# Moving products apart: an attention pair in the mixing stage and the second routing of a mixture-of-experts kernel on one Trainium2 core

## The chip, the cores and the metric

The kernel runs on 1 core of one Trainium2 chip. The time is device microseconds of one execution; three executions of the kernel before gave 1412.86, 1415.44 and 1416.71 us, median 1415.44. One more execution was recorded by the profiler. PE is TensorE's matmul stream, PEld its weight loads, DVE is VectorE, ACT is ScalarE, POOL is GpSimd, SP is SyncE, which here only issues DMAs.

## The reference, cut to what matters

```python
# q,k,v: [8, 8, 576, 64]; p: [8, 8, 32, 64]
pp  = softmax(p k^T / 8) v ;  a = softmax(q pp^T / 8) pp          # x = a as [8, 576, 512]
u   = x + real(fft(fft(x, axis=1), axis=2))                       # sequence, then channels
un  = (u - mean(u)) / sqrt(var(u) + 1e-6)
x   = u + relu(un @ w_ch1) @ w_ch2                                # 512 -> 2048 -> 512, the "mixing" stage
logits = x @ w_gate ; keep = sigmoid(x @ w_local) >= 0.5          # 8 experts
e[s] = e[s-1] if keep[s] and s > 0 else argmax(logits[s])         # a scan along the sequence
out[s] = softmax(logits[s])[e[s]] * (relu(x[s] @ w1[e]) @ w2[e])  # 512 -> 1024 -> 512, expert e only
```

Float32 products are made of three float16 ones (high by high, high by low, low by high: the list `PASS`).

## The kernel before, in words

**Mixing.** The eight batch rows are mixed one after another (`full(b)`, 512 of the 576 places each), and the remaining 64 places of four rows are mixed together as `R0` and `R1` (`half`). The order is 0, 1, 2, R0, 3, 4, 5, 6, R1, 7. A mix has 16 slices f: `mm1(f)` makes twelve products of 512 columns into a bank `hp`, which ACT and DVE split into halves `ht`; `mm2(f-2)` makes twelve into the accumulators `acc`. `mm1` reads the whole transposed input `UT[b]` from its first product on.

**What runs beside it.** Python generators hand out the other work in steps, one step per `yield`. `tick` is called after every third product of a full mix (a sub-tick) and advances each generator in the list `bg` by 0.25 times its rate. While mix b runs, `attention(b+1)` is handed out at rate 2.3, `last`, which is `after_mix` of the mix before (scale, halves, transpose, logits), at rate 1.2, and `expert_weights` (casts of the expert weights) at 1.3. `attention` has some 60 steps and a mix 112 sub-ticks for it; what is left is drained before the next mix begins. The tile scheduler orders the instructions of each engine by program order as priority and by readiness in its own timing model, so an instruction can be issued ahead of its place in the program. Each engine then works its instructions in the order given.

**The pair of products in question.** In `attention`, `products(cs, hf, tiles)` makes the cosine (cs 0) or sine (cs 1) product of one group of 128 columns hf into a bank `bp`. Products(0,0,...) and products(0,1,...), six matmuls each, stand in one step. `att` banks come from the pool `psA`, which has two; the logits of `after_mix` use the same pool (`lp`, read by DVE at L1208 into `lsum`). After the products the step order is halves, `zd`, three output tiles t with products `P`, `Q`, `X`, and `norm`, whose four transposed tiles are sent by DMA into `UT` (L724). Output tile 2 fills a quarter of the shared tile; its `P` and `X` hold both `att` banks.

**Routing.** The first routing (`gr` 0) runs in mix 7 and covers half of the places. The second (`finish_routing`: `after_mix` of mix 7 by TensorE transposes, then `routing(1)` = `choose` and `place`) runs at rate 1.2 beside the first expert turns. In an expert turn `e1` (96 products of 128 columns, 8 ticks) and `e2` (24 products of 512 columns, 8 ticks) alternate over consecutive blocks. `choose` sends `ff` products (places to rows, L1286 to L1293), a scan on DVE, `ep` products (L1310, L1314); `place` sends `tt` and `rk` (L1351, L1352), some 34 small DVE operations, and then nine chunks of DVE comparisons, each followed by four `tab` products (L1465). The second routing has to be done when the seventh turn begins (`drain(r1)`).

**Buffers.** `hl` has three slots in SBUF, which the rows gathered for expert blocks (`xg`) and the halves `xh` of `after_mix` share; `U` has eight, for the mixes' outputs and the experts' results `ys`.

Of the kernel before, what the change touches and what calls it, by code (L numbers as in the profile page):

```python
# [192 lines left out]
def _build(tc, nc, ctx, A, stop):  # L193
# [152 lines left out]
    def attention(b):  # L346
# [237 lines left out]

        for hf in range(2):
            products(0, hf, (0, 1))
        yield
        for hf in range(2):
            products(0, hf, (2,))
# [608 lines left out]
    def after_mix(tiles, by_pe=False):  # L1198
        xt = None

        def logits(col):
            lp = att(f"lp{col}")
            for c in range(4):
                nc.tensor.matmul(lp[:, :18], xt[:, c], wgh[:, c].rearrange("p y e -> p (y e)"), start=c == 0, stop=False,
                                 skip_group_check=True)
                nc.tensor.matmul(lp[:, :9], xt[:, 4 + c], wgh[:, c, 0], start=False, stop=c == 3, skip_group_check=True)
            lsum = wp.tile([128, 9], F32, tag="lsum", name=f"lsum{col}", bufs=2)
            nc.vector.tensor_reduce(lsum, lp[:, :18].rearrange("p (y e) -> p e y", y=2), axis=AX.X, op=ALU.add)  # L1208
            nc.vector.tensor_scalar(LG[:, col], lsum, RSC[:, col:col + 1], 2.0 ** -20, ALU.mult, ALU.mult)

        for j, (ut, col) in enumerate(tiles):
            sc = wp.tile([128, 2], F32, tag="rsc", name=f"rsc{col}", bufs=2)
            nc.vector.tensor_reduce(sc[:, 0:1], ut, axis=AX.X, op=ALU.max, apply_absolute_value=True)
            nc.vector.tensor_scalar(RSC[:, col:col + 1], sc[:, 0:1], 1e-30, 0.25, ALU.max, ALU.mult)
            nc.vector.reciprocal(sc[:, 1:2], RSC[:, col:col + 1])
            yield
            hl = wp.tile([128, 1024], F16, tag="hl", name=f"xh{col}", bufs=3)
            nc.scalar.activation(hl[:, :512], ut, AF.Copy, scale=sc[:, 1:2])
            nc.vector.scalar_tensor_tensor(hl[:, 512:], ut, sc[:, 1:2], hl[:, :512], ALU.mult, ALU.subtract)
            yield  # L1220
            if j:
                yield
                logits(tiles[j - 1][1])
                yield
            xt = wp.tile([128, 8, 128], F16, tag="xt", name=f"xt{col}", bufs=1)
            if by_pe:
                for x in range(2):
                    turn_half(xt[:, 4 * x:4 * x + 4], hl[:, 512 * x:512 * x + 512], f"xtp{col}_{x}", x)
            else:
                nc.sync.dma_start_transpose(out=xt, in_=hl)  # L1230
            nc.sync.dma_start(XS[128 * col:128 * col + 128], hl)
            yield
        for _ in range(1 if by_pe else 4):
            yield
        logits(tiles[-1][1])
        yield


    def wait(n):
        for _ in range(n):  # L1240
            yield

    def choose(gr, rp):

# [28 lines left out]
        for k in range(2):  # L1273
            nc.vector.tensor_tensor(mr[:, k], fk[:, k, 16:18].unsqueeze(2).to_broadcast([128, 2, 4]),
                                    rmask.unsqueeze(1).to_broadcast([128, 2, 4]), op=ALU.mult)
        yield from wait(2)
        fs = rp.tile([4, 2, 576], F16, tag="fs", name=f"fs{gr}")
        for k in range(2):
            for lu in range(2):
                ps = att(f"ff{gr}_{k}_{lu}")  # L1280

                def sel(t):
                    return fk[:, k, 0:16].rearrange("p (b s) -> p s b", s=4)[:, 2 * t + lu]

                if lu == 0:
                    nc.tensor.matmul(ps[:4, 0:128], sel(0), idh, start=True, stop=True, skip_group_check=True)  # L1286
                    nc.tensor.matmul(ps[:4, 128:256], sel(1), idh, start=False, stop=True, skip_group_check=True)
                    nc.tensor.matmul(ps[:4, 256:288], mr[:, k, 0], i32r, start=False, stop=True, skip_group_check=True)
                else:
                    nc.tensor.matmul(ps[:4, 33:161], sel(1), anti, start=True, stop=True, skip_group_check=True)  # L1290
                    nc.tensor.matmul(ps[:4, 161:288], sel(0), anti[:, :127], start=False, stop=True, skip_group_check=True)
                    nc.tensor.matmul(ps[:4, 0:1], sel(0), anti[:, 127:128], start=False, stop=True, skip_group_check=True)
                    nc.tensor.matmul(ps[:4, 1:33], mr[:, k, 1], i32v, start=False, stop=True, skip_group_check=True)  # L1293
                if k:
                    nc.vector.tensor_copy(fs[:, k, 288 * lu:288 * lu + 288], ps[:4, :288])
                else:
                    nc.scalar.copy(fs[:, k, 288 * lu:288 * lu + 288], ps[:4, :288])
            yield
# [4 lines left out]
        rev = bass.AP(tensor=src.tensor, offset=src.offset + 575, ap=[src.ap[0], [-1, 287]])  # L1303
        nc.vector.tensor_copy(e16[:, 1, 1:288], rev)
        nc.vector.tensor_copy(e16[:, 1, 0:1], e16[:, 0, 288:289])
        yield from wait(2)
        ep = att(f"ep{gr}")
        for t in range(2):
            for lu in range(2):
                nc.tensor.matmul(ep[:, 4 * (2 * t + lu):4 * (2 * t + lu) + 4], e16[:, lu, 128 * t:128 * t + 128],  # L1310
                                 idh[:4, :4], start=t + lu == 0, stop=True, skip_group_check=True)
        for q in range(4):
            for lu in range(2):
                nc.tensor.matmul(ep[32 * q:32 * q + 32, 16 + lu:17 + lu], e16[:, lu, 256:288], idh[:4, q:q + 1],  # L1314
                                 start=False, stop=True, skip_group_check=True)
        nc.vector.tensor_copy(EXP[:, c0:c0 + 16].rearrange("p (b k) -> p b k", k=4),
                              ep[:, 0:16].rearrange("p (k b) -> p b k", b=4))
# [10 lines left out]
        nc.vector.tensor_scalar(sm, sm, 1e-9, None, ALU.add)  # L1328
        nc.vector.reciprocal(sm, sm)
        nc.vector.tensor_tensor(d, d, OH[:, c0:c0 + 18], op=ALU.mult)  # L1330
        pe = t18("pe")
        nc.vector.tensor_reduce(pe, d, axis=AX.X, op=ALU.add)
        nc.vector.tensor_tensor(pe, pe, sm, op=ALU.mult)
        val, pc = VAL[:, c0:c0 + 18], PIECES[:, c0:c0 + 18]
        nc.vector.scalar_tensor_tensor(val, pe, 2.0 ** -28, RSC[:, c0:c0 + 18], ALU.mult, ALU.mult)
        nc.scalar.copy(pc[:, :, 0:4], c32[:, 420:564].rearrange("p (i c) -> p c i", i=4)[:, c0:c0 + 18])
        for i in range(4, 7):
            nc.vector.tensor_copy(pc[:, :, i], val)
# [4 lines left out]
    def place(nm, ncol, b0, nb, early, rp):  # L1343
# [4 lines left out]
        rk = att(f"rk{nm}")  # L1348
        tt = att(f"tt{nm}")
        ohf = oh.rearrange("p c e -> p (c e)")  # L1350
        nc.tensor.matmul(tt[:, :n8], ones, ohf, start=True, stop=True)  # L1351
        nc.tensor.matmul(rk[:, :n8], tri, ohf, start=True, stop=True)  # L1352
        tot = rp.tile([128, 8, 36], F32, tag="tot", name=f"tot{nm}")
        inc = rp.tile([128, 8, 36], F32, tag="inc", name=f"inc{nm}")
        if ncol < 36:
# [100 lines left out]
        nc.vector.tensor_scalar(pi, pi, 7, None, ALU.arith_shift_right)  # L1456
        nc.vector.tensor_copy(blk[:, 0, :ncol], pi)
        nc.vector.scalar_tensor_tensor(blk[:, 1, :ncol], blk[:, 0, :ncol], -128.0, pos, ALU.mult, ALU.add)
        yield from wait(4)

        tab = att(f"tab{nm}")
        made = []

        def table(c, ow, bv):
            nc.tensor.matmul(tab[:, :7 * nb].rearrange("p (i n) -> p i n", i=7), ow, bv[:, :, :nb],  # L1465
                             start=c == 0, stop=c == ncol - 1)

        for c0 in range(0, ncol, CT):
            cs = slice(c0, min(c0 + CT, ncol))
# [9 lines left out]
            nc.vector.tensor_tensor(ow[:, :n], iota.unsqueeze(1).to_broadcast([128, n, 128]),  # L1479
                                    blk[:, 1, cs].unsqueeze(2).to_broadcast([128, n, 128]), op=ALU.is_equal)  # L1480
            made.append((c0, n, ow, bv))
            yield
            if c0:
                m0, mn, ow, bv = made[-2]
                for i in range(mn):
# [39 lines left out]

    w1b, w2b = [], []
    xg, xt, regs, hb = {}, {}, {}, {}
    newest = [None]

    def load_x(b):  # L1530
        mp = M["p"]
# [36 lines left out]
    def e1(b, todo=(), beside=iter(())):  # L1568
# [3 lines left out]
        for fg in range(2):  # L1572
            hp = (psM, psO)[fg].tile([128, 512], F32, tag="ho"[fg], name=f"ehp{b}_{fg}")
            for f in range(4):
                n = 0
                cols = slice(128 * f, 128 * f + 128)
                for c in range(4):
                    for (x, y) in PASS:
                        newest[0] = nc.tensor.matmul(hp[:, cols], w1b[r][:, 2 * c + fg, x, cols], xt[b][:, 4 * y + c],  # L1579
                                                     start=n == 0, stop=n == 11, skip_group_check=True).ins  # L1580
                        n += 1
                if f % 2 == 0:
                    for fn, t in todo:
                        fn(t, 2 * fg + f // 2, 2 * fg + f // 2 + 1)
                if f % 2:
                    next(beside, None)
                if f < 3:
                    tick()
            nc.scalar.activation(ht[:, fg, 0], hp, AF.Relu)  # L1589
            nc.vector.scalar_tensor_tensor(ht[:, fg, 1], hp, 0.0, ht[:, fg, 0], ALU.max, ALU.subtract)  # L1590
            tick()
# [32 lines left out]
    def e2(b, todo=()):  # L1624
# [5 lines left out]
        for f in range(8):  # L1630
            for (x, y) in PASS:
                for a in range(2 if two else 1):
                    rows = slice(64 * a, 64 * a + 64) if two else slice(0, 128)
                    c0 = 128 * (f % 4)
                    nc.tensor.matmul(op[rows], h[:, f // 4, x, c0 + rows.start:c0 + rows.stop], w2b[r + a][:, f, y],  # L1635
                                     start=n == 0, stop=n == 23, skip_group_check=True)
                n += 1
            if f % 2 == 0:
                for fn, t in todo:
# [157 lines left out]
```

## Time and profile before

| what | value |
|---|---|
| median of three executions | 1415.44 us (1412.86 to 1416.71) |
| profiled execution | 1416.94 us, its span 1414.9 us |
| PE busy | 1368.8 us, 97% of the span |
| PEld busy | 790.2 us, 56% |
| DVE, ACT, POOL busy | 702.1, 518.4, 376.0 us |
| TensorE's granted clock | 0.991 of full speed over the span |

The span is what the profile's rows cover; the profiled execution's time is 2.0 us more. A window row gives a stretch's busy times by engine, a timeline row one instruction or a run of equal ones with its start and length, and in square brackets the idle time of the engine ahead of it with what ended it. A matmul's row is longer than the distance to the next one, because matmuls are pipelined; their rate is read from the starts of consecutive rows.

### The profile page before, as it was taken

How to read it: one execution, taken by the hardware profiler on the slowest of the kernel's cores; microseconds unless marked ns; L12 is line 12 of the kernel's file. 1: busy time of each engine (PE TensorE's matmuls, PEld its weight loads, DVE VectorE, ACT ScalarE, POOL GpSimd, SP SyncE). 2: the span in 40 equal slices, each digit the busy share in tenths (PEclk: the TensorE clock that was granted, in tenths of full speed). 3: DMA queues.
4: the chain of work that ended last, by engine and by line, in shares of the span. 5: the costliest groups of instructions: out<-in, count | busy, mean ns of one | idle time of the engine just before them, and what ended most of it. 6: DMA issues, size and time to landing. Idle time of an engine off the chain costs nothing. (4 is left out here: it accounts for less than half of the span.)

```text
span 1414.9 us, 27811 instructions
## 1 busy us (share of the span) xinstructions
PE 1368.8 (97%) x10868; PEld 790.2 (56%) x10868; DVE 702.1 (50%) x1420; ACT 518.4 (37%) x953; POOL 376.0 (27%) x386
## 2 busy tenths in 40 slices
PE   7999899999999999999999999999899999999998
PEld 5653444444564544444444456445677777776565
DVE  5899957657544655655655655443751111111111
ACT  2543365455445545445445444211211111111112
POOL 1102243443422443343343342000211121122101
PEclk7999999999999999999999999999999999999999
DMA  7475384684567657557557446243949669957883
GB/s 263 141 253 168 100 238 121 169 235 122 142 175 202 164 137 212 158 140 217 151 131 217 126 134 173 67 179 113 284 126 301 192 183 252 264 142 238 236 250 140
DMA packets 219640, 256.62 MB, mean 181 GB/s; under 512 B 151663, under 2 KB 163055, under 8 KB 216816
## 3 DMA queue, kind: packets, MB, share of 16 engines
q1 hardware_dynamic: 213424, 235.39, 58.9%
q0 software_dynamic: 6080, 19.40, 4.1%
q8 instruction: 87, 1.43, 0.4%
q14 instruction: 49, 0.40, 0.1%
HBM read 267.52 MB, written 52.95 MB: 226 GB/s over the span
## 5 line engine op out<-in xcount | busy, mean ns | idle before, releaser
L1176 PE MATMUL acc<-w,ht 128*128 128x512 f16 x1728 | 411.0, 379 | 1.0 <-ACT ht L1163 0.8
L1156 PE MATMUL hp<-ut,w 128*128 128x512 f16 (+1 forms) x1536 | 366.1, 379 | 2.2 <-DMA ut<-unh 1.6
L1156 PEld LDWEIGHTS <-w 128*128 128x128 f16 x1920 | 182.6, 98 | 180.5 <-issue 10.9
L1176 PEld LDWEIGHTS <-ht 128*128 128x128 f16 x1728 | 165.4, 98 | 190.4 <-issue 8.5
L339 POOL TENSOR_TENSOR halfs<-stage,halfs 128x512 f16<-128x512 f32 x128 | 150.5, 1181 | 298.7 <-ACT halfs L338 280.1
L1635 PE MATMUL eo<-w2b,hx 128*128 128x512 f16 (+1 forms) x984 | 207.5, 379 | 0.1
L1579 PE MATMUL ehp<-xgt,w1b 128*128 128x128 f16 x3360 | 202.6, 219 | 1.1 <-PE ehp L1579 0.8
L1579 PEld LDWEIGHTS <-w1b 128*128 128x128 f16 x3360 | 192.6, 98 | 16.5 <-issue 3.8
L1590 DVE SCALAR_TENSOR_TENSOR hx<-ehp,hx 128x512 f16<-128x512 f32 x70 | 48.2, 689 | 269.4 <-ACT hx L1589 255.7
L1164 DVE SCALAR_TENSOR_TENSOR ht<-hp,ht 128x512 f16<-128x512 f32 (+1 forms) x160 | 101.1, 632 | 149.6 <-ACT ht L1163 148.6
L1163 ACT ACTIVATE ht<-hp 128x512 f16<-128x512 f32 (+1 forms) x160 | 88.0, 550 | 238.3 <-PE hp L1156 233.4
L1635 PEld LDWEIGHTS <-hx 128*128 128x128 f16 (+1 forms) x984 | 87.3, 100 | 95.3 <-issue 3.5
L1644 POOL DMA_INDIRECT out<-ys,sidx x38 | 38.2, 1006 | 290.4 <-ACT ys L1643 268.9
L1589 ACT ACTIVATE hx<-ehp 128x512 f16<-128x512 f32 x70 | 41.8, 597 | 155.5 <-PE ehp L1579 155.5
L1643 ACT ACTIVATE ys<-eo,scl 128x512 f32<-128x512 f32 x38 | 26.1, 687 | 155.5 <-PE eo L1635 155.5
L338 ACT CAST halfs<-stage 128x512 f16<-128x512 f32 x128 | 77.6, 615 | 9.2 <-DMA WS<-halfs 5.4
L337 ACT ACTIVATE stage<-stage 128x512 f32<-128x512 f32 x128 | 77.7, 623 | 0.2
L1534 POOL DMA_INDIRECT xg<-XS,gidx x38 | 39.7, 1045 | 140.9 <-DVE sidx L1500 52.1
L364 POOL TENSOR_TENSOR qh<-q,qh 128x1420 f16<-128x1420 f32 x12 | 34.6, 2883 | 51.0 <-ACT qh L363 50.9
L1156 PE MATMUL hp<-utr,w 128*128 128x256 f16 x384 | 47.1, 272 | 0.0
L541 POOL TENSOR_TENSOR eo<-ee 128x256 f32<-128x256 f32 (+1 forms) x21 | 18.6, 887 | 74.3 <-DVE ee L525 71.1
L576 PE MATMUL bp<-cst,eh 128*128 128x289 f16 (+1 forms) x168 | 25.5, 286 | 11.5 <-DVE lsum L1208 9.8
(413 smaller groups left out, 1404.0 us busy)
## 6 DMA issues: line engine op xcount, KB each, us to landing
w1b<-WS SPq DMA_DIRECT2D x156, 512.0 KB
w2b<-WS SPq DMA_DIRECT2D x156, 512.0 KB
stage<-in_w SPq DMA_DIRECT2D x64, 512.0 KB
WS<-halfs SPq DMA_DIRECT2D x128, 256.0 KB
q<-in_qd SPq DMA_DIRECT2D x16, 710.0 KB
v<-in_vd SPq DMA_DIRECT2D x16, 640.0 KB
k<-in_kd SPq DMA_DIRECT2D x16, 576.0 KB
XS<-xh SPq DMA_DIRECT2D x36, 256.0 KB
```

What stands on the lines that cost most here:

```text
L337: nc.scalar.activation(st[:, a], st[:, a], AF.Copy, scale=64.0 if k < 4 else 256.0)
L338: nc.scalar.copy(so[:, 0], st[:, a])
L339: nc.gpsimd.tensor_tensor(so[:, 1], st[:, a], so[:, 0], op=ALU.subtract)
L1156: nc.tensor.matmul(hp[:, c0:ntok], w12[:, f, 0, x, 128 * c:128 * c + 128], ut[:, 4 * y + c, c0:ntok], start=n == 0, stop=n == 11, skip_gro ...
L1163: pace[1] = nc.scalar.activation(ht[:, 0, :ntok], hp[:, :ntok], AF.Relu).ins
L1164: pace[0] = nc.vector.scalar_tensor_tensor(ht[:, 1, :ntok], hp[:, :ntok], 0.0, ht[:, 0, :ntok], ALU.max, ALU.subtract).ins
L1176: nc.tensor.matmul(self.acc[j], ht[:, x, 128 * j:128 * j + 128], w12[:, f, 1, y], start=f == 0 and n == 0, stop=f == 15 and n == 2)
L1534: nc.gpsimd.indirect_dma_start(out=g_, out_offset=None, in_=XS[0:rows], in_offset=bass.IndirectOffsetOnAxis(ap=gidx[:, b:b + 1], axis=0), ...
L1579: newest[0] = nc.tensor.matmul(hp[:, cols], w1b[r][:, 2 * c + fg, x, cols], xt[b][:, 4 * y + c], start=n == 0, stop=n == 11, skip_group_ch ...
L1589: nc.scalar.activation(ht[:, fg, 0], hp, AF.Relu)
L1590: nc.vector.scalar_tensor_tensor(ht[:, fg, 1], hp, 0.0, ht[:, fg, 0], ALU.max, ALU.subtract)
L1635: nc.tensor.matmul(op[rows], h[:, f // 4, x, c0 + rows.start:c0 + rows.stop], w2b[r + a][:, f, y], start=n == 0, stop=n == 23, skip_group_ ...
```

## The change

In `attention`, from batch row 2 on, two empty steps stand between the first pair of products. In `after_mix` of the last mix, the halves take slots of the pool `U` in place of `hl`. In the second routing, more empty steps stand ahead of `ff`, `ep` and the tables, two in place of one after each chunk, and each of its products (`ff`, `ep`, `tt`, `rk`, `tab`) gets an ordering edge, without a semaphore, behind the expert product that was written last at that point of the program (`latest`). The first routing keeps its steps. In the diff below, the first two `wait` lines stand ahead of `ff` and of `ep`, the third ahead of the tables, and the last one after each chunk; `pe` then stands in place of `nc.tensor` in those products.

```diff
         for hf in range(2):
             products(0, hf, (0, 1))
+            if hf == 0 and b >= 2:
+                yield from wait(2)
...
-            hl = wp.tile([128, 1024], F16, tag="hl", name=f"xh{col}", bufs=3)
+            if by_pe:
+                hl = wp.tile([128, 512], F32, tag="U", name=f"xh{col}", bufs=8).bitcast(F16)
+            else:
+                hl = wp.tile([128, 1024], F16, tag="hl", name=f"xh{col}", bufs=3)
...
+    class in_line:
+        def __init__(self, late):
+            self.late = late
+        def matmul(self, *a, **k):
+            with tc.issue_after(latest[0]) if self.late and latest[0] is not None else nullcontext():
+                nc.tensor.matmul(*a, **k)
...
-        yield from wait(2)
+        yield from wait(6 if gr else 2)
...
+                pe = in_line(gr)
...
-        yield from wait(2)
+        yield from wait(5 if gr else 2)
         ep = att(f"ep{gr}")
+        pe = in_line(gr)
...
+        pe = in_line(not early)
...
-        yield from wait(4)
+        yield from wait(4 if early else 16)
...
-            yield
+            yield from wait(1 if early else 2)
...
-                        newest[0] = nc.tensor.matmul(hp[:, cols], w1b[r][:, 2 * c + fg, x, cols], xt[b][:, 4 * y + c],
+                        newest[0] = latest[0] = nc.tensor.matmul(hp[:, cols], w1b[r][:, 2 * c + fg, x, cols], xt[b][:, 4 * y + c],
...
-                    nc.tensor.matmul(op[rows], h[:, f // 4, x, c0 + rows.start:c0 + rows.stop], w2b[r + a][:, f, y],
+                    latest[0] = nc.tensor.matmul(op[rows], h[:, f // 4, x, c0 + rows.start:c0 + rows.stop],
```

## Rows read from the trace of the kernel before

**Rows 1.** Windows: length, busy us (instructions) of PE, PEld, DVE, ACT, POOL; clock, DMA.
```profile
525.40:632.00 106.60, 103.24 (x701) 51.58 (x700) 65.39 (x127) 54.59 (x102) 40.98 (x39) 1.00 0.64 169
983.30:1045.00 61.70, 57.24 (x700) 42.74 (x699) 50.23 (x147) 13.82 (x24) 9.67 (x9) 1.00 0.85 248
```

**Rows 2.** Waits of PE over the span: us in total, times, longest.
```profile
PE bp L576 <- DVE lsum L1208: 9.8, 5, 2.7
```

**Rows 3.** Timeline around the pair of attention(2): start, us, engine, line, operation.
```profile
227.54 2.15 DVE L539 SCALAR_TENSOR_TENSOR eo<-ee,c 99x256 f32<-99x256 f32 x1
...
229.62 0.91 PE L576 MATMUL bp<-cst,eh 128*128 128x289 f16 x6
...
231.48 0.68 DVE L1164 SCALAR_TENSOR_TENSOR ht<-hp,ht 128x512 f16<-128x512 f32 x1
...
232.08 0.17 DVE L1208 TENSOR_REDUCE lsum<-lp 128x9 f32<-128x18 f32 x1
...
232.30 0.90 PE L576 MATMUL bp<-cst,eh 128*128 128x289 f16 x6 [1.77 <-DVE lsum L1208]
```

**Rows 4.** Timeline around the pair of attention(5).
```profile
588.08 0.91 PE L576 MATMUL bp<-cst,eh 128*128 128x289 f16 x6
...
591.43 0.17 DVE L1208 TENSOR_REDUCE lsum<-lp 128x9 f32<-128x18 f32 x1
...
591.65 0.91 PE L576 MATMUL bp<-cst,eh 128*128 128x289 f16 x6 [2.67 <-DVE lsum L1208]
```

**Rows 5.** Timeline of PE around the start of mix 2.
```profile
260.55 0.82 PE L644 MATMUL X<-pph,big 128*128 128x256 f16 x6
...
263.15 2.75 PE L1176 MATMUL acc<-w,ht 128*128 128x512 f16 x12
265.74 2.75 PE L1156 MATMUL hp<-ut,w 128*128 128x512 f16 x12
...
272.73 0.38 PE L1156 MATMUL hp<-ut,w 128*128 128x512 f16 x1
```

**Rows 6.** Timeline of PE at the start of mix 6.
```profile
738.13 0.38 PE L1156 MATMUL hp<-ut,w 128*128 128x512 f16 x1
```

**Rows 7.** Timeline of SP's DMA issues ahead of mix 2 and of mix 6.
```profile
268.10 2.62 SPq L724 DMA_TRANSPOSE ut<-unh  x2
...
733.49 3.72 SPq L724 DMA_TRANSPOSE ut<-unh  x2
```

**Rows 8.** Timeline of PE around the start of mix 1.
```profile
162.95 0.82 PE L644 MATMUL X<-pph,big 128*128 128x256 f16 x6
...
166.63 4.71 PE L1176 MATMUL acc<-w,ht 128*128 128x512 f16 x21
...
173.21 0.69 PE L385 MATMUL s<-k,p 64*32 64x288 f32 x8 [1.88 <-DVE ru L676]
...
175.49 3.15 PE L1156 MATMUL hp<-ut,w 128*128 128x512 f16 x7 [1.58 <-DMA ut<-unh]
```

**Rows 9.** Timeline of PE in the second routing.
```profile
1001.95 0.17 PE L1206 MATMUL lp<-wgh,xt 128*128 128x9 f16 x1
...
1005.42 0.22 PE L1286 MATMUL ff<-c,fk 128*4 128x128 f16 x1 [0.60 <-DVE fk L1269]
...
1009.69 0.17 PE L1310 MATMUL ep<-c,e 4*128 4x4 f16 x1 [1.20 <-DVE e L1300]
...
1011.55 0.29 PE L1351 MATMUL ttf<-OH,c 128*128 128x288 f16 x1
...
1023.67 0.60 PE L1465 MATMUL tabf<-stage,owf 128*128 128x238 bf16 x4 [1.68 <-DVE stage L1476]
...
1025.54 0.58 PE L1465 MATMUL tabf<-stage,owf 128*128 128x238 bf16 x4
...
1027.41 0.59 PE L1465 MATMUL tabf<-stage,owf 128*128 128x238 bf16 x4
```

**Rows 10.** Timeline of ACT in the second routing.
```profile
994.62 0.72 ACT L1218 ACTIVATE xh<-ul,rsc 128x512 f16<-128x512 f32 x1 [0.60 <-DMA XS<-xh]
```

More of the change, by code (lines that the diff above doesn't have):

```diff
@@ L1285, in choose @@
                 if lu == 0:
-                    nc.tensor.matmul(ps[:4, 0:128], sel(0), idh, start=True, stop=True, skip_group_check=True)
-                    nc.tensor.matmul(ps[:4, 128:256], sel(1), idh, start=False, stop=True, skip_group_check=True)
-                    nc.tensor.matmul(ps[:4, 256:288], mr[:, k, 0], i32r, start=False, stop=True, skip_group_check=True)
-                else:
[L1290 to L1293, printed above, removed]
+                    pe.matmul(ps[:4, 0:128], sel(0), idh, start=True, stop=True, skip_group_check=True)
+                    pe.matmul(ps[:4, 128:256], sel(1), idh, start=False, stop=True, skip_group_check=True)
+                    pe.matmul(ps[:4, 256:288], mr[:, k, 0], i32r, start=False, stop=True, skip_group_check=True)
+                else:
+                    pe.matmul(ps[:4, 33:161], sel(1), anti, start=True, stop=True, skip_group_check=True)
+                    pe.matmul(ps[:4, 161:288], sel(0), anti[:, :127], start=False, stop=True, skip_group_check=True)
+                    pe.matmul(ps[:4, 0:1], sel(0), anti[:, 127:128], start=False, stop=True, skip_group_check=True)
+                    pe.matmul(ps[:4, 1:33], mr[:, k, 1], i32v, start=False, stop=True, skip_group_check=True)
                 if k:
@@ L1305, in choose @@
         nc.vector.tensor_copy(e16[:, 1, 0:1], e16[:, 0, 288:289])
-        yield from wait(2)
+        yield from wait(5 if gr else 2)
         ep = att(f"ep{gr}")
+        pe = in_line(gr)
         for t in range(2):
             for lu in range(2):
-                nc.tensor.matmul(ep[:, 4 * (2 * t + lu):4 * (2 * t + lu) + 4], e16[:, lu, 128 * t:128 * t + 128],
+                pe.matmul(ep[:, 4 * (2 * t + lu):4 * (2 * t + lu) + 4], e16[:, lu, 128 * t:128 * t + 128],
                                  idh[:4, :4], start=t + lu == 0, stop=True, skip_group_check=True)
@@ L1313, in choose @@
             for lu in range(2):
-                nc.tensor.matmul(ep[32 * q:32 * q + 32, 16 + lu:17 + lu], e16[:, lu, 256:288], idh[:4, q:q + 1],
+                pe.matmul(ep[32 * q:32 * q + 32, 16 + lu:17 + lu], e16[:, lu, 256:288], idh[:4, q:q + 1],
                                  start=False, stop=True, skip_group_check=True)
@@ L1330, in choose @@
         nc.vector.tensor_tensor(d, d, OH[:, c0:c0 + 18], op=ALU.mult)
-        pe = t18("pe")
-        nc.vector.tensor_reduce(pe, d, axis=AX.X, op=ALU.add)
-        nc.vector.tensor_tensor(pe, pe, sm, op=ALU.mult)
+        pm = t18("pm")
+        nc.vector.tensor_reduce(pm, d, axis=AX.X, op=ALU.add)
+        nc.vector.tensor_tensor(pm, pm, sm, op=ALU.mult)
         val, pc = VAL[:, c0:c0 + 18], PIECES[:, c0:c0 + 18]
-        nc.vector.scalar_tensor_tensor(val, pe, 2.0 ** -28, RSC[:, c0:c0 + 18], ALU.mult, ALU.mult)
+        nc.vector.scalar_tensor_tensor(val, pm, 2.0 ** -28, RSC[:, c0:c0 + 18], ALU.mult, ALU.mult)
         nc.scalar.copy(pc[:, :, 0:4], c32[:, 420:564].rearrange("p (i c) -> p c i", i=4)[:, c0:c0 + 18])
@@ L1350, in place @@
         ohf = oh.rearrange("p c e -> p (c e)")
-        nc.tensor.matmul(tt[:, :n8], ones, ohf, start=True, stop=True)
-        nc.tensor.matmul(rk[:, :n8], tri, ohf, start=True, stop=True)
+        pe = in_line(not early)
+        pe.matmul(tt[:, :n8], ones, ohf, start=True, stop=True)
+        pe.matmul(rk[:, :n8], tri, ohf, start=True, stop=True)
         tot = rp.tile([128, 8, 36], F32, tag="tot", name=f"tot{nm}")
@@ L1464, in table @@
         def table(c, ow, bv):
-            nc.tensor.matmul(tab[:, :7 * nb].rearrange("p (i n) -> p i n", i=7), ow, bv[:, :, :nb],
-                             start=c == 0, stop=c == ncol - 1)
+            in_line(not early).matmul(tab[:, :7 * nb].rearrange("p (i n) -> p i n", i=7), ow, bv[:, :, :nb],
+                                      start=c == 0, stop=c == ncol - 1)
         for c0 in range(0, ncol, CT):
@@ L1527, in _build @@
     xg, xt, regs, hb = {}, {}, {}, {}
-    newest = [None]
+    newest, latest = [None], [None]
     def load_x(b):
@@ L1634, in e2 @@
                     c0 = 128 * (f % 4)
-                    nc.tensor.matmul(op[rows], h[:, f // 4, x, c0 + rows.start:c0 + rows.stop], w2b[r + a][:, f, y],
-                                     start=n == 0, stop=n == 23, skip_group_check=True)
+                    latest[0] = nc.tensor.matmul(op[rows], h[:, f // 4, x, c0 + rows.start:c0 + rows.stop],
+                                                 w2b[r + a][:, f, y], start=n == 0, stop=n == 23,
+                                                 skip_group_check=True).ins
                 n += 1
```

## The prediction

> **What bounds the kernel now.** I read the windows by stage first. In a mix with its attention PE is busy 103.24 of 106.60 us, no other engine more than 65.4, and the DMA share is 0.64 [rows 1]. Whether a busy PE is also a PE at its rate is read from starts: twelve 512-column products run from 263.15 to the next row at 265.74, 2.59 us or 216 ns each, at a granted clock of 1.00, the 2.4 GHz level [rows 1, 5]; 512 columns at that clock are 213 ns. So what PE does cannot shrink here, and what can be won is the time in which it waits. The list of PE's waits has one large entry that recurs: the second products of the pair wait for `lsum`, 9.8 us in five waits, the longest 2.7 [rows 2]. The timelines show how. The logits of the mix before hold one of two `att` banks; the first of the pair takes the other; the second needs the bank that DVE frees with `lsum`, and that stands in DVE's queue behind L539 and L1164 of this mix [rows 3]. PE's products come in order, so the mix products behind the pair stand too, though their inputs are there: 1.77 us in attention(2), 2.67 in attention(5) [rows 3, 4]. Third, the window of the second routing: PE is busy 57.24 of 61.70 us at full clock, so 4.5 us are idle [rows 1]. Three waits make 3.48 of it: 0.60 for `ff`, 1.20 for `ep`, 1.68 for the first table [rows 9].
>
> A rule that speaks against this reading: the Trainium skill, "Perfetto Trace Analysis", section "Identifying the Most-Contended Engine", says that matmul busy time is a poor measure of closeness to the limit and wants the weight loads' busy share and the achieved rate instead. The weight loads are busy 51.58 of 106.60 us, 48% [rows 1], which by that measure leaves PE half free; but the 216 ns per product agree with the section's other measure, the rate, that PE is at its limit while it is busy.
>
> **The pair in attention.** Nothing is removed and nothing is added to any engine; six matmuls, and all attention behind them, move by two steps. A sub-tick hands out 2.3 x 0.25 = 0.575 steps and comes after three products, 3 x 0.216 = 0.65 us. Two steps are 2 / 0.575 = 3.48 sub-ticks or 2.25 us of PE work, in whole sub-ticks three or four, 1.95 or 2.6 us. That work is the rest of a slice's `mm1` and the start of an older `mm2`, both with inputs long there: the halves `ht` of DVE's row at 231.48 are wanted only by the slice after next. The bank is freed on DVE's time, which the pair doesn't set. So a wait shorter than 2 us goes whole: 1.77, and the three that lie between, whose sum is 9.8 - 1.77 - 2.67 = 5.4 us, so 1.8 on average. The 2.67 leaves 0.1 to 0.7. I take 0.5 for all that remains: 9.3 us gained. Bounds: 0 (if `lsum` is put off as far as the pair is) and 9.8. If the cover fails, it costs what it costs now. In attention(4) there is no such wait, and nothing is gained there.
>
> **What is late next: the input of the next mix.** Everything behind the pair in attention(b) moves toward the end of the mix by those 2.25 us of PE work, and the mix's end does not move. In mix 1 the last `X` of tile 1 runs at 260.55 and the next mix's first product at 272.73, 12.18 us later [rows 5]. Between them the norm chain goes through DVE, POOL, DVE, ACT and POOL, and its last transposes are issued by 268.10 + 2.62 = 270.72 [rows 7], 2.01 us before the first product that needs them. Ahead of mix 6 it is 733.49 + 3.72 = 737.21 to 738.13, 0.92 us [rows 6, 7]; four mixes (2, 4, 5 and 6) have this form, the other two between these ends. In mixes 3 and 7 the half mix stands between and takes its own input. No row shows the landing of a transpose there; since mix 6 did not wait, it is between 0 and 0.92 us behind the issue. With 0, the slack of 2.01 and 0.92 against a shift of 2.25 gives waits of 0.24 in three and 1.33 in one, 2.1 us in all. With 0.92 it gives 1.16 in three and 2.25 in one, 5.7 us. The planner can also put older `mm2` products (twelve, 2.59 us) ahead, and the wait is then 0; at the start of mix 1 it did so with some of the 21 `acc` products at 166.63, and PE still waited 1.88 and 1.58 us [rows 8]. I take 3.5 us: between 2.1 and 5.7, since the rows of mixes 2 and 6 show the plain order, and below their middle of 3.9, since the planner may lift some of it. Bounds: 0 and 4 x 3.46 = 13.8, the pattern of mix 1 four times. Tile 2's `P` and `X`, which hold both banks, move too, and with them the next scores; these are ready work for PE that the planner can shift, and I count them inside that range. Behind a transpose that comes late on SP stand only the casts' stores and loads, for which no row shows PE waiting. The two idle steps hold an open bank 2.25 us longer; the next logits need one some 17 sub-ticks (11 us) after the last, so they don't meet.
>
> Sum for the mixes: 9.3 - 3.5 = 5.8 us gained.
>
> **The second routing.** The products are the same; they are pinned to the places where the program writes them, which moves further back. A step at rate 1.2 is 0.65 / 1.2 = 0.54 us (an estimate from the same 0.65 us a tick). From the last logits to `ff` there were 3 steps, 1.6 us; there will be 7, 3.8 us. Their distance in the trace is 1005.42 - 1001.95 = 3.47 us [rows 9], set by DVE: covered. From the first `ff` to `ep` the trace has 4.27 us [rows 9]; there will be 7 steps and some 0.8 us of `ff` themselves, 4.6: covered. From `tt` to the first table 12.12 us [rows 9]; there will be 22 steps, 11.9: 0.2 short. Chunks of DVE work follow each other at 1027.41 - 1025.54 = 1.87 us [rows 9]; four steps are 2.2, three were 1.6. So of 3.48 us nearly all goes; I allow 0.7 for pinned products that meet DVE late, since the planner can no longer shift them: 2.8 us gained. Bounds: 4.5, all that idles there, and a loss of 2 us, if every one of the three meets its input as late as the mean of these waits again and one more. The later end costs nothing: the routing has some 89 steps, 74 ticks, which is over in the fifth turn, and the seventh needs it.
>
> **The buffers.** The third and fourth `xh` wait for a DMA that frees an `hl` slot, 0.60 us on ACT for the third [rows 10]; in `U` the four slots of mix 6 are free by then, and the first `ys` comes after the mix-7 outputs are read. This brings the logits forward, which the pinning then places; in PE's idle time it is worth 0 to 0.5 us, and I count 0.
>
> **Sum.** 5.8 + 2.8 = 8.6 us. The profiled execution took 1416.94 us, 1.50 above the median; 1416.94 - 8.6 = 1408.3, and against the median 1415.44 the forecast is 1406.8 us.
>
> **Rivals.**
> All covered: the planner finds work for the late inputs, so the mixes give 9.3 and the routing 3.3, 12.6 in all: 1402.8 us. For it: at the start of mix 1 it did pull `mm2` products forward. Against it: its model misjudged the same chain there by 3.5 us [rows 8]. Chance 0.20.
> Given back: the plain order is kept and each of the four mixes waits the whole 2.25 us, 9.0; the mixes gain 0.3, the routing 1: 1414.1 us. For it: ahead of mix 6 the slack is only 0.92 us. Against it: three others have about 2. Chance 0.14.
> Slower: the late end of attention becomes in four mixes what it is ahead of mix 1, where the banks held by tile 2 stop the next scores (1.88) and the input stops the products (1.58): 4 x 3.46 = 13.8 us against 9.3, and the pinned products lose 1 in place of winning: 1415.44 + 5.5 = 1420.9 us. It decides from a wait of (9.3 + 2.8) / 4 = 3.0 us a mix. For it: the end of attention then stands one step from the drain. Against it: mix 1's chain also had four DVE additions of the mix before in it, which later ones have not. Chance 0.06.
> The wait moves with the pair: `lsum` is freed later too, or PE takes the same idle time elsewhere, and the routing gains nothing: 1415.4 us. Against it: DVE's queue ahead of `lsum` holds nothing of what is moved. Chance 0.06.
> The forecast itself has 0.54.
>
> **How the numbers follow.** The forecast's own range, from its two largest unknowns (0 to 5.7 at the mixes' starts, 1.5 to 3.5 in the routing), is 1403 to 1410. The range given is 1402.0 to 1413.0: it takes in the first rival and stops short of the others, which hold 0.26, of which I count a quarter inside since "given back" can be partial. A measurement of this kernel tells about 0.3% (4.2 us) from no change, so faster means below 1411.2. Faster: 0.54 + 0.20 and 0.02 of a partial second rival, 0.76. Same: 0.12 + 0.06, 0.18. Slower: 0.06.
>
> **What would show it.** Right: the `lsum` entry among PE's waits falls from 9.8 us to under 1.5; between the pair stand nine to twelve mix products; the waits of `ff`, `ep` and the first table fall below 1 us together; new PE waits for `ut` at the starts of mixes 2, 4, 5 and 6 sum to about 3.5 us. Wrong: an `lsum` wait that is still there behind the moved products, waits of over 3 us at those starts, or new waits of PE for DVE in the routing.

## Result, and the profile after

The changed kernel takes 1401.94 us (median of 6, 1399.4 to 1406.91) against 1414.6 us (6 runs, 1411.27 to 1416.71) of the kernel before in the same sessions: ratio 0.9913, 95% interval 0.9893 to 0.9932. That is 12.3 us less (9.6 to 15.1), where 8.6 were forecast. The profiled execution has a span of 1400.3 us.

PE's waits after the change (us in total, times, longest) answer to [rows 2]:

```profile
PE pps L440 <- DMA et<-ehl: 1.8, 2, 1.1
...
PE hp L1158 <- DMA ut<-unh: 1.6, 1, 1.6
PE pps L440 <- DVE vhl L430: 1.6, 2, 1.3
PE bp L576 <- DVE big L582: 1.4, 1, 1.4
...
PE pps L440 <- ACT vhl L428: 1.2, 1, 1.2
...
PE bp L576 <- DVE lsum L1210: 0.7, 1, 0.7
...
PE hp L1158 <- DVE ht L1166: 0.6, 1, 0.6
```

The same view of the kernel before had, for the lines that grew or stayed:

```profile
PE hp L1156 <- DMA ut<-unh: 1.6, 1, 1.6
...
PE pps L440 <- DMA et<-ehl: 1.3, 1, 1.3
...
PE pps L440 <- DVE vhl L430: 0.5, 1, 0.5
```

The `lsum` entry went from 9.8 to 0.7 us. The wait for `ut` is the one at the start of mix 1, the same before and after; none came at the later mixes. But `pps`, products early in the next attention, wait 4.6 us where it was 1.8, and waits for the evacuations `big` and `ht` add 2.0.

The timeline of PE around the pair of attention(2) shows nine mix products between the two, and no wait [rows 3]:

```profile
222.86 0.91 PE L576 MATMUL bp<-cst,eh 128*128 128x289 f16 x6
223.60 1.46 PE L1158 MATMUL hp<-ut,w 128*128 128x512 f16 x6
224.90 0.81 PE L1178 MATMUL acc<-w,ht 128*128 128x512 f16 x3
225.55 0.91 PE L576 MATMUL bp<-cst,eh 128*128 128x289 f16 x6
```

The second routing, timeline of PE and a window of the same length from the first expert product on: no bracket stands at `ff`, `ep`, `tt` or the first table [rows 9], and 0.93 us of 61.70 are idle where it was 4.46 [rows 1].

```profile
992.38 0.27 PE L1256 MATMUL ff<-c,fk 128*4 128x128 f16 x2
...
997.37 0.39 PE L1256 MATMUL ep<-c,e 4*128 4x4 f16 x12
999.04 0.29 PE L1256 MATMUL ttf<-OH,c 128*128 128x288 f16 x1
...
1011.64 0.38 PE L1256 MATMUL tabf<-stage,owf 128*128 128x238 bf16 x2
```
```profile
973.22:1034.92 61.70, 60.77 (x784) 47.58 (x783) 51.01 (x148) 14.88 (x26) 9.24 (x7) 1.00 0.77 236
```

**Two stretches that can be compared.** The profiles differ by some 7 us at the start and 4 us at the end, so the experiments below are also read by two stretches of their one profile, which leave both out: the mixes, from the first `bp` of attention(1) to the first expert product, and the routing, from there to the first `eo` product of the seventh turn. The mixes hold one more difference: in some executions PE's granted clock falls to the lower level, 1.2 GHz, for part of a few microseconds, always after PE has idled for some. The clock column adds up, over windows of 5 us, the clock's shortfall times the window's length, which is what it can have cost at most; "less clock" leaves it out.

| kernel | mixes us | clock us | less clock | routing us |
|---|---|---|---|---|
| before | 857.9 | 3.4 | 854.5 | 89.5 |
| changed | 852.0 | 1.7 | 850.3 | 83.9 |
| e1 pair only | 852.3 | 1.7 | 850.6 | 89.6 |
| e2 routing only | 854.3 | 0 | 854.3 | 83.5 |
| e3 six steps | 866.3 | 5.2 | 861.2 | 83.6 |
| e4 read first | 857.7 | 1.7 | 856.0 | 89.7 |
| e5 changed again | 851.8 | 1.7 | 850.1 | 83.6 |
| e6 skip attention(4) | 849.3 | 1.7 | 847.6 | 83.8 |
| e7 logits early | 846.2 | 0 | 846.2 | 83.6 |
| e8 no edges | 852.2 | 1.7 | 850.5 | 84.0 |
| e9 buffers only | 856.2 | 1.8 | 854.4 | 87.7 |
| e10 no buffers | 849.5 | 0 | 849.5 | 86.0 |

The routing stretch repeats within 0.5 us in kernels with the same routing, the mixes less clock within 1.7 in kernels with the same attention. The mean of the mixes less clock is 854.8 us in the four kernels with the pair together and the old rate of the logits (before, e2, e4, e9) and 850.2 in the five with the changed attention (changed, e1, e5, e8, e10). So the change is worth some 4.6 us in the mixes and 5.6 in the routing.

### The profile page after: what moved, and what is told of

It reads as the page before. It is cut to its first block, busy times and chain, and to the rows that moved or that the text cites. A ratio compares the mean times of both kernels' runs of the same rounds, so it can differ in the third digit from the quotient of the medians.

```text
span 1400.3 us, 27806 instructions
## 1 busy us (share of the span) xinstructions
PE 1362.5 (97%) x10868; PEld 787.5 (56%) x10868; DVE 704.1 (50%) x1420; ACT 516.8 (37%) x953; POOL 377.9 (27%) x386
## 4 chain that ended last, share of the span: by engine, by line
PE 55%; DVE 3%; issue 1%; DMA 1%; ACT 0%; POOL 0%; POOLq 0%; DVEq 0%; ACTq 0%; SPq 0%
PE eo L1653 13%; PE ehp L1597 13%; PE acc L1178 11%; PE hp L1158 11%; PE ehp L1622 1%; PE bp L576 1%; PE X L646 1%; DMA xt<-xh 0%; DVE rsc L1215 0%; PE P L636 0%; DMA out<-ys,sidx 0%; PE s L503 0%; PE s L385 0%; PE pps L440 0%; PE P L641 0%
## 5 line engine op out<-in xcount | busy, mean ns | idle before, releaser
L724 POOL TENSOR_TENSOR unh<-un,unh 128x512 f16<-128x512 f32 x28 | 31.8, 1158 | 18.3 <-ACT unh L723 15.9
```

## Experiments

**One part alone.** The pair's two empty steps on the kernel before:

```diff
             products(0, hf, (0, 1))
+            if hf == 0 and b >= 2:
+                yield from wait(2)
```

> The kernel before with the two empty steps between the pair of products and nothing else. Theory (the pair's wait was PE's own time, and the mixes' inputs have room): PE's lsum wait falls from 9.8 us to under 1, no new wait for ut, the time is 8 to 10 us below the kernel before, and the second routing still idles PE some 4 us. Rival (the gain of the changed kernel comes mostly from the routing, or from PE's clock in single executions): 0 to 4 us below.

Ratio 0.9953 (0.9933 to 0.9974), 6.6 us less (3.7 to 9.5); `lsum` waits 0.7 us, but `pps` 6.0. And the other part, which is the changed kernel less those two lines:

> The changed kernel without the two empty steps in attention: the second routing's part and the buffers alone. Theory: lsum wait stays at 9 to 10 us, PE idles under 1.5 us in the second routing in place of 4.5, the time is 3 to 4 us below the kernel before. Rival (it carries most of the gain): 8 us or more below.

Ratio 0.9956 (0.9938 to 0.9973), 6.2 us less (3.8 to 8.8); `lsum` waits 9.8 us as before. Neither number is what its theory or its rival said: the pair gave less than 8 to 10 by its median, though its interval reaches into that range, and the routing between 3 to 4 and 8. Together they make up the 12.3 us.

**Where the rest of the pair's gain went.** First the place that the forecast had named, with the pair pushed further:

```diff
-                yield from wait(2)
+                yield from wait(6)
```

> The changed kernel with six empty steps in place of two, a shift of 6 / 0.575 x 0.65 = 6.8 us. Theory A (the forecast took slice 15 of the old mix for the first products of the new one; the last transposes have 9.4 us before they are needed): still no wait for ut, time within 3 us of the changed kernel, some 12 us below before. Theory B (the room is the 0.9 to 2 us of the forecast, and the planner or a shorter chain made up for two steps): 4 to 6 us of waits at each of four mixes less up to 2.6 that the planner can lift, so 8 to 20 us above the changed kernel.

Ratio 1.0026 (1.0011 to 1.0041): slower than before. By the two ratios it is some 16 us above the changed kernel, and 13.7 above it by the medians, which come from different sessions. The total fits theory B and the parts fit neither. Timeline of SP and PE at the start of mix 2, PE's wait list over the span and a window behind the start of mix 2:

```profile
269.65 2.61 SPq L726 DMA_TRANSPOSE ut<-unh  x2
```
```profile
265.72 2.75 PE L1158 MATMUL hp<-ut,w 128*128 128x512 f16 x12
...
274.13 1.05 PE L1158 MATMUL hp<-ut,w 128*128 128x512 f16 x3 [2.19 <-DMA ut<-unh]
275.11 1.18 PE L385 MATMUL s<-k,p 64*32 64x288 f32 x8
```
```profile
PE hp L1158 <- DMA ut<-unh: 8.3, 4, 2.3
...
PE hp L1158 <- issue: 2.3, 1, 2.3
```
```profile
275.00:280.00 5.00, 5.00 (x28) 1.39 (x27) 1.23 (x4) 0.27 (x1) 0.00 (x0) 0.70 0.21 72
```

The input is late by some 2.2 us at each of the four mixes (2.19, 2.22, 2.26 and 2.28, together 9.0), not by 4 to 6. In the list, the first line holds three of them and the 1.6 us of mix 1; the second line is the fourth, at mix 6, where the trace names no releaser but the transposes stand on SP as they do at the others. Behind three of these waits the clock's mean over 5 us falls to 0.70, 0.68 and 0.75, and the shortfall makes up to 5.2 us of the loss. The rows give what none of before showed: PE goes on 274.13 - 272.26 = 1.87 us after the issue of the last transpose ended (269.65 + 2.61 = 272.26).

Theory A named the right row and still had no wait in it, and the rows say why. Counted from the first product of mix 1 (171.30 us in the changed kernel, 174.66 here), the last transposes are issued 4.4 us later than in the changed kernel. And in the changed kernel the 32 score products of the next attention (L385) run ahead of the mix's first product; here they are late themselves and come behind it, from 275.11 on, so that without its wait the mix would begin 2.6 us earlier. Both together use up the 4.9 us that the changed kernel had to spare (worked out below) and 2.1 more.

Then the kernel before, without moving a product, with DVE's read of the logits at the priority of `ht`:

```diff
-            nc.vector.tensor_reduce(lsum, ...)
+            with tc.high_priority(offset=URGENT):
+                nc.vector.tensor_reduce(lsum, ...)
```

> The kernel before, products where they were, but DVE's read of the logits (lsum) gets the higher priority that the halves ht have, so that it stands earlier in DVE's queue. Theory (the second product waits only because the read that frees its bank stands late in DVE's queue): PE's lsum wait falls from 9.8 us to under 3 without any product being moved, 6 to 9 us below before. Rival (the bank is late for another reason, or the read ahead makes the halves late in turn): the wait stays above 6 us, or the same time turns up as PE waits for ht; within 2 us of before.

Ratio 1.0001 (0.9982 to 1.0019), and it tells nothing: DVE's order did not change, the read still stands behind `ht`. What an earlier read alone would give stays untested.

```profile
227.77 0.68 DVE L1164 SCALAR_TENSOR_TENSOR ht<-hp,ht 128x512 f16<-128x512 f32 x1
228.37 0.17 DVE L1209 TENSOR_REDUCE lsum<-lp 128x9 f32<-128x18 f32 x1
```

The next three ran beside each other.

> The changed kernel itself, beside the next two runs. Both theories: 11 to 13 us below before; PE waits for lsum under 1 us, for vhl ahead of the pps products of attention(5) 2 to 2.5 us.

Ratio 0.9902 (0.9886 to 0.9919), 13.9 us less than before; `lsum` 0.8 us; ahead of `pps` of attention(5) 2.2 us. The waits are there again, this time without the dip of the clock at 555 us.

```diff
-            if hf == 0 and b >= 2:
+            if hf == 0 and b >= 2 and b != 4:
```

> The changed kernel, but attention(4) keeps its pair together, where no lsum wait stood. Theory (the two steps push the end of attention(4), so the scores and loads of attention(5) come later, SP and ACT are held up and vhl is late for pps): the pps waits of attention(5) fall from 2.5 us to 0.5 as before, the dip of the granted clock behind them at 550 to 560 us is gone, 2 to 4 us below the changed kernel. Rival (vhl is late because PE is earlier, not because attention(4) ended later): the pps waits stay at 2 us or more, within 1 us of the changed kernel.

Ratio 0.9883 (0.9865 to 0.9901); the median is 1398.78 us against 1401.67. The two intervals overlap, so the reading rests on the mixes, which are 2.5 us shorter than those of e5, and on the waits. Of its list of waits the `pps` lines:

```profile
PE pps L440 <- DMA et<-ehl: 1.2, 2, 1.0
PE pps L440 <- DVE vhl L430: 0.8, 2, 0.5
```

No `pps` product of attention(5) waits 0.3 us or more now. So the later end of attention(4), which itself had no `lsum` wait to gain, is what made attention(5) late. How it gets there is read from timelines of PE, in the changed kernel and then in e6. The rows are the last scores of attention(5), its first `pps` products and its second ones:

```profile
522.80 1.17 PE L385 MATMUL s<-k,p 64*32 64x288 f32 x16
...
545.59 1.03 PE L440 MATMUL pps<-vhl,et 128*64 128x128 f16 x30
...
552.49 0.25 PE L440 MATMUL pps<-vhl,et 128*64 128x128 f16 x2 [1.23 <-ACT vhl L428]
...
554.02 0.97 PE L440 MATMUL pps<-vhl,et 128*64 128x128 f16 x28 [1.28 <-DVE vhl L430]
```
```profile
524.09 1.17 PE L385 MATMUL s<-k,p 64*32 64x288 f32 x16
...
549.26 1.03 PE L440 MATMUL pps<-vhl,et 128*64 128x128 f16 x30
...
554.85 1.36 PE L440 MATMUL pps<-vhl,et 128*64 128x128 f16 x30
```

The first `pps` products stand behind four slices of the mix in both. The scores stand 25.17 us ahead of them in e6 and 22.79 in the changed kernel: they moved by 2.4 us, and `pps` did not. What lies between came with the scores. ACT's second `vhl` ends 29.6 us after the scores in both. On the way ACT, which takes its work in order, stands still for the load of q, 4.90 us in the changed kernel and 2.67 in e6 (timeline of ACT, same order):

```profile
538.24 1.37 ACT L363 CAST qh<-q 128x1420 f16<-128x1420 f32 x1 [4.90 <-DMA q<-in_qd]
```
```profile
539.68 1.38 ACT L363 CAST qh<-q 128x1420 f16<-128x1420 f32 x1 [2.67 <-DMA q<-in_qd]
```

On SP that load is issued behind transposes that need the scores (in the changed kernel at 532.71 us, behind the one at 530.46). That this order is what makes it late is read from the queue, and no run tried it by itself.

**Moving the bank's holder and not the pair.** The routing part, the pair left together, and the logits earlier:

```diff
-LAST_RATE = 1.2
+LAST_RATE = 1.35
```

> The routing part and the buffers, the pair left together as before, but the generator of the logits runs at rate 1.35 in place of 1.2, so that the third logits come some 6 sub-ticks (4 us) ahead of the pair instead of one. Theory (the bank that the logits hold is the whole cause, and moving the logits costs attention nothing): lsum wait under 1.5 us, pps waits as before (under 1.5 us in all), the mixes 8 to 10 us shorter than with the routing part alone, 13 to 16 us below before. Rival (the logits then meet other holders of the two banks, the scores above all): new waits of PE for banks of 4 us or more, not faster than the changed kernel.

Ratio 0.9861 (0.9842 to 0.9879), 19.7 us less than before; median 1394.76 us against 1401.67 of the changed kernel beside it. Timelines of PE and DVE around the pair of attention(2), and its `pps` and `bp` waits:

```profile
215.92 0.17 PE L1204 MATMUL lp<-wgh,xt 128*128 128x18 f16 x1
...
220.66 1.65 PE L576 MATMUL bp<-cst,eh 128*128 128x289 f16 x12
```
```profile
219.97 0.16 DVE L1208 TENSOR_REDUCE lsum<-lp 128x9 f32<-128x18 f32 x1
```
```profile
PE pps L440 <- DMA et<-ehl: 0.8, 1, 0.8
...
PE pps L440 <- DVE vhl L430: 0.7, 1, 0.7
...
PE bp L576 <- DVE big L582: 0.4, 1, 0.4
```

The logits are sent 4.7 us ahead of the pair, the bank is free 0.5 us before it is wanted, and the twelve products run in one piece. `bp` has no `lsum` entry any more, `pps` waits 1.5 us, and the mixes are 846.2 us, 8.1 below those of e2 and 4.1 below the changed kernel's less clock. So the held bank is the cause of the pair's wait, and moving its holder costs attention little: `pps` waited 0.9 us in e2, and the new small waits (`big` 0.4 and two of 0.3 to 0.4) stand against one of 1.3 us for `gp` that is gone as well. DVE still reads the logits late, 3.7 us after they were made; that now ends before the pair begins. The rival's 4 us of bank waits did not come. The gain of 19.7 us is more than the 13 to 16 expected: the two stretches hold some 14 of it, with the clock left out, and the rest is not explained. Of the kernels tried this has the lowest time; its interval lies clear of that of the changed kernel beside it, and overlaps that of e6.

**What in the routing did it.** The changed kernel without its ordering edges (`self.late = False`):

> The changed kernel with the later steps of the second routing but without the ordering edges. Theory (the edges do the work, since the planner lifts the products to where its own timing model has their inputs ready): PE waits for ep, ff and the first table stay near 3 us in all, and the first eight expert blocks take some 89 us as before in place of 84. Rival (the later steps alone do it): waits under 1 us, 84 us.

1406.05 us, one run, 4.4 above the median of e5; its two stretches are within 0.4 us of those of e5. The rival is right: the waits of `ep`, `ff` and the first table are gone, the stretch is 84.0 us, and the distances are those of the changed kernel, 12.52 us from `tt` to the first table against 12.60:

```profile
1002.44 0.29 PE L1256 MATMUL ttf<-OH,c 128*128 128x288 f16 x1
...
1014.96 0.38 PE L1256 MATMUL tabf<-stage,owf 128*128 128x238 bf16 x2
```

The kernel before with the pool `U` for the last halves and nothing else, and the changed kernel with `hl`:

```diff
-            hl = wp.tile([128, 1024], F16, tag="hl", name=f"xh{col}", bufs=3)
+            if by_pe:
+                hl = wp.tile([128, 512], F32, tag="U", name=f"xh{col}", bufs=8).bitcast(F16)
+            else:
+                hl = wp.tile([128, 1024], F16, tag="hl", name=f"xh{col}", bufs=3)
```

> The kernel before with the last tiles' halves in the pool U and nothing else. From the first expert product to the start of the seventh turn's second layer the kernel before takes 89.5 us and the changed kernel 83.9. Theory (the buffers are worth little by themselves, the later steps carry it): 88 to 90 us, the waits of ep, ff and the first table still some 3 us in all. Rival (the halves' wait for an hl slot sets the routing's pace, and the steps only keep it): 84 to 86 us.

> The changed kernel with the last tiles' halves back in hl. The same stretch. Theory (the later steps carry it): 84 to 86 us, with PE waiting for ff up to 1.5 us since the logits end later. Rival (the buffers carry it): 87 to 90 us.

One run each, 1405.97 and 1400.46 us, with 1409.69 for one run of the kernel before beside them. The routing stretch is 87.7 us, just under what the theory of e9 said, and 86.0, at the edge of what the theory of e10 said: the buffers alone take 1.8 us off, the steps alone 3.5, both 5.6, so they add, within the 0.5 us by which the stretch repeats. The waits of PE in the stretch, first of the buffers alone, then of the steps alone, say which is whose:

```profile
PE tabf L1468 <- DVE stage L1479: 1.8, 2, 1.6
PE ep L1313 <- DVE e L1303: 0.6, 1, 0.6
```
```profile
PE xtp L1194 <- ACT xh L1220: 1.8, 2, 1.5
PE ff L1253 <- DVE fk L1283: 0.4, 1, 0.4
```

The steps remove the table's wait, the buffers the transposes' wait for `xh` and with it the wait for `ff` and half of the one for `ep` [rows 9].

## Why the prediction was right and where it failed

- **What bounds the kernel.** Right. PE's waits taken away came back as time, to the size that the stretches show.
- **The pair.** Right in mechanism and size: 9.3 us of waits were to go, 9.8 - 0.7 = 9.1 did. Nine products stand between the two, as foreseen. The three waits not shown in the rows were 1.56, 2.21 and 1.55 us, so two of them did not lie between 1.77 and 2.67; that changed nothing, as all three went.
- **What is late next: the input of the next mix.** This step failed. The forecast took the `hp` row at 272.73 [rows 5] for the first product of mix 2. It belongs to slice 15 of mix 1. The changed kernel's timelines of SP and PE show it: the row that answers to it starts before the issue of the transposes has ended.

```profile
261.84 2.62 SPq L726 DMA_TRANSPOSE ut<-unh  x2
```
```profile
263.10 1.46 PE L1158 MATMUL hp<-ut,w 128*128 128x512 f16 x6
...
268.80 1.18 PE L385 MATMUL s<-k,p 64*32 64x288 f32 x16
...
271.22 2.75 PE L1158 MATMUL hp<-ut,w 128*128 128x512 f16 x12
```

The six at 263.10 and six more behind them are slice 15, and the mix begins with the next twelve, at 271.22; in e3 the twelve at 265.72 are slice 15 and the next `hp` product waits for `ut`. In the kernel before, mix 2 begins at this row of PE's timeline:

```profile
280.09 2.75 PE L1156 MATMUL hp<-ut,w 128*128 128x512 f16 x12
```

With the 1.87 us of landing from e3 the room was 280.09 - 270.72 - 1.87 = 7.5 us, not 0 to 2; after two steps it is 271.22 - 264.46 - 1.87 = 4.9, and nothing waits. The room is not slack of a fixed size: part of it is made by the scores that run ahead of the mix, and it went when they came late (e3). What probably misled was these scores: they have a raised priority, run beside slice 15, and make the place look like the start of the next mix. The 3.5 us set down for four mixes' starts were 0.
- **What was late next in fact.** Waits inside the attentions: `pps` 1.8 to 4.6 us, `big` 1.4 and `ht` 0.6 new, 4.8 in all against 3.5 at the wrong place. So the mixes' net, 9.1 - 4.8 = 4.3 us by the waits and 4.6 by the stretch, came near the forecast's 5.8 by luck, with the cause misnamed. The forecast did say that the next scores would move, and counted them as ready work. For attention(5) they weren't free: the chain from the scores to `vhl` moved with them, `pps` did not, and e6 shows that the two steps in attention(4), where the forecast saw nothing to gain and counted no loss, were the cause. The new wait for `big` stands in attention(3), ahead of its next `bp` products (1.41 us at 334.24), and takes back most of the 1.56 that the pair gave there. What made it and `ht` late was not followed up.
- **The second routing.** The mechanism was right and the term too small: 2.8 us forecast, 5.6 in the stretch. Of that, 1.8 is the buffers, which were costed at 0: their wait stood in PE's idle time as a late chain, and with the buffers alone the 0.60 for `ff` is gone and the 1.20 for `ep` is 0.6 (e9). The idle time of the same window fell from 4.46 to 0.93 us, 3.53, and 5.6 were won: a matmul's row covers part of the gap behind it. The pair shows by how much: the first row is 0.91 us long [rows 3] while the next products start 0.74 us later when nothing holds them (222.86 to 223.60), so a wait shown as 1.77 us was 1.94. That every small wait of the routing is short by such an amount is an inference.
- **The edges.** The forecast took them for what holds the products at their later places. The later steps alone do that; without the edges the stretch is the same within its 0.5 us (e8, one run).
- **The rivals.** The forecast time was 1406.8 us and "all covered" 1402.8; the measured ratio lies at the latter, by luck. Its reason, that the planner finds work for late inputs, is not what happened, since no input was late at the four starts in question. "Slower" and "given back" did not come, but the first appears at six steps (e3), with the clock as part of its price, which the forecast had left out.

## What to carry to other kernels

When a product waits for a shared bank, look at who holds it. Moving the holder by 4 us cost little and gave 8 us, while moving the waiting work shifted everything behind it and gave half. Before a slack is worked out from a row, make sure whose row it is: count the rows of a repeated stage up to it, or check that its inputs could have been there. Work that runs ahead only because it is ready makes room that goes when that work comes late. And read idle time in pipelined rows as a lower bound.

## What was not expected of the hardware

After some of PE's waits its granted clock was at the lower level for part of the next few microseconds, and after similar waits in other executions it was not. The waits of attention(5) around 550 us, in two pieces, add up to 2.5 us in the changed kernel and in e8 and to 3.3 in e1, and the mean clock over 5 us fell to 0.66, 0.78 and 0.72; in e5 and e10 they are 2.2 and 2.1 us, and no dip follows. The waits of 1.9 and 1.6 us at the start of mix 1 stand in all twelve profiles, and a dip follows in five of them (before, e4, e5, e6, e9). The 2.67 us wait of the kernel before [rows 4] had none. In e3 a dip follows three of the four waits at the mixes' starts; that cost up to 5.2 us beside the 9.0 of the waits themselves.
